# A pitch of 68 KB in place of 64 KB in two DRAM scratch tensors

## The chip, the cores and the metric

The kernel runs on one core of one Trainium2 chip. The metric is the device time of one execution in microseconds, the median of three runs. Lower is better. A profile of one more execution of each kernel gives the spans, the waits and the DMA packets.

## The reference

Each of 8 batches has 3008 rows of 256 numbers. A real Fourier transform runs along the rows, a complex 256 x 256 weight with a bias and a soft threshold is applied to every frequency, and the inverse transform goes back. Then a two-layer network with an ELU follows on all 24064 rows:

```python
X = np.fft.rfft(x, axis=1)
Yr = Xr @ w_r - Xi @ w_i + b_r
Yi = Xr @ w_i + Xi @ w_r + b_i
Yr, Yi = soft(Yr, 0.01), soft(Yi, 0.01)     # sign(v) * max(|v| - 0.01, 0)
y = np.fft.irfft(Yr + 1j * Yi, n=3008, axis=1)
h = y.reshape(24064, 256) @ w_in            # 256 -> 2048
out = elu(h) @ w_out                        # 2048 -> 256
```

## The kernel before

The length 3008 is split as 47 x 64, so each transform is done in two steps of matrix products with a change of layout between them. The layout is changed by way of DRAM: a tile with 128 partitions is stored, and read back with other numbers on the partitions.

For a batch `b` the work is a row of units:

- `unit_A` (6 units of 4 columns j): the first step of the forward transform. `load_x` has brought a third of the batch into `xts[ci]`; two matrix products with `M1` fill PSUM, a copy makes bf16 tile `A`, and a store on the SP queue writes it to the scratch tensor `DA` of shape [24, 128, 256] bf16. One row of 256 is 512 bytes, one j is 64 KB. The stores take 4 j each in batch 0 (line 154) and 8 j later (line 156); every partition writes one 512-byte row for each j.
- `load_Z` reads `DA` back as `Z` with 96 partitions: each j is cut into 4 runs of 32 rows, and every run lands on one partition. The DRAM side folds j and the quarter into one count of 96 with a step of 16 KB. Batch 0 uses four loads of 8 rows per partition (384 KB, pieces of 4096 bytes); the later batches use one of 8 rows and one of 24 rows (1152 KB, pieces of 12288 bytes). Line 163.
- `unit_X` (8 units): the second step, from `Z` and `M2` into `XT`. Units 2g and 2g+1 need rows 8g to 8g+7 of `Z`.
- `unit_M` (12 units) applies the weights, the bias and the threshold; `unit_B` (6 units) is the first step of the inverse transform and stores `Bz` to the scratch tensor `DB`, again [24, 128, 256] (lines 254 and 259).
- `load_Bs` reads `DB` back as four tiles `Bs` of 96 partitions with 8 rows each (384 KB, line 265), and `unit_Y` (8 units, two for each `Bs`) makes the transposed rows `yT` in SBUF.

The network runs over blocks of 512 rows with 8 pairs of 128 hidden columns each, 376 steps in all. A step has `front` (the product with `w_in_s`, line 695, and the exponential), `elu` and `finish_elu` on VectorE, and, two steps later, `back` (the product with `w_out_r`, line 752). After each block the result goes through `osb` to the output (line 770); where the block crosses a quarter of a batch, the store of 16 runs of 8 rows is cut in two, with 14 and 2 runs, 12 and 4, and so on.

The order is written out by hand. Batch 0 goes first, alone, with filler products (`idle_pe`) on TensorE; the A units of batch 1 follow, and its `Z` loads. From then on `plan(b)` gives each step at most one unit of the next batches, behind which the step's own network products stand: the last Y units of batch b, the X, M and B units of batch b+1, the A units of batch b+2, then the loads of `Z` for b+2. Every engine runs its instructions in program order. All scratch stores, scratch loads and output stores are issued on the SP queue in program order too; loads of x and `w_out` go through the GpSimd queue. `gate` holds back the loads of x until a part of `Z` has landed.

The two scratch tensors come from a DRAM pool with two buffers each.

Of the kernel before, what the change touches and what calls it, by code (L numbers as in the profile page):

```python
# [10 lines left out]
BF16 = mybir.dt.bfloat16  # L11
# [10 lines left out]
K1 = 24  # L22
NH = N2 // 2
NJ = 24
# [5 lines left out]
def kernel(  # L30
# [11 lines left out]
    nc = tc.nc  # L42
    P = nc.NUM_PARTITIONS

    B, S, D = x.shape
# [30 lines left out]
    dram = ctx.enter_context(tc.tile_pool(name="dram", bufs=2, space=bass.MemoryType.DRAM))  # L76
# [16 lines left out]
    LAG = 2  # L93
    n = B * PER
    WT = 2 * N1 * 8


    A_of = {}
    DA_of = {}
    Z_of = {}  # L100
# [3 lines left out]
    DB_of = {}  # L104
# [12 lines left out]
    def unit_ps(name, alone):  # L117
        if alone:
            return pre2.tile([P, 2, 512], F32, name=name, tag="pre2")
        return psF.tile([P, 2, 512], F32, name=name, tag="fps")  # L120

    def evac(dst, src, on_dve):
        if on_dve:
            nc.vector.tensor_copy(dst, src)
        else:
            nc.scalar.copy(dst, src)  # L126

    def unit_A(b, u, alone=False, on_dve=False, ahead=False):
        ci, uu = u // 2, u % 2
        if uu == 0:  # L130
            if ahead and ci > 0:
                A_of[b, ci] = late3.tile([P, 8, D], BF16, name="A", tag="gT")
            elif alone:
                A_of[b, ci] = wk4.tile([P, 8, D], BF16, name="A", tag="Bs")
            else:
                A_of[b, ci] = wk2.tile([P, 8, D], BF16, name="A", tag="A")
            if ci == 0:
                DA_of[b] = dram.tile([NJ, P, D], BF16, name="DA", tag="DA")
        xt, A = xts[ci], A_of[b, ci]
        dav = DA_of[b].rearrange("j p d -> p j d")  # L140
        ps = unit_ps("aps", alone or ahead)
        for j in range(2):
            nc.tensor.matmul(  # L143
                ps[:, j, :], lhsT=M1[:],
                rhs=xt[:, 4 * uu + 2 * j : 4 * uu + 2 * j + 2, :], start=True, stop=True,
            )
        evac(
            A[:, 4 * uu : 4 * uu + 4, :].rearrange("p n d -> p (n d)"),
            ps[:].rearrange("p a b -> p (a b)"), on_dve,
        )  # L150
        j0 = 8 * ci
        if alone:
            j0 += 4 * uu
            nc.sync.dma_start(dav[:, j0 : j0 + 4, :], A[:, 4 * uu : 4 * uu + 4, :])
        elif uu == 1:
            nc.sync.dma_start(dav[:, j0 : j0 + 8, :], A[:])

    def load_Z(b, s0, s1):

        if b not in Z_of:  # L160
            Z_of[b] = zp.tile([2 * NR, NS, D], BF16, name="Z", tag="Z")
        dv = DA_of[b].rearrange("j (h c s) d -> (j h c) s d", h=2, c=2)
        nc.sync.dma_start(Z_of[b][:, s0:s1, :], dv[:, s0:s1, :])

    def unit_X(b, u, alone=False, on_dve=False):
        g, dt = u // 2, u % 2
# [60 lines left out]
    def unit_B(b, v, alone=False, on_dve=False):  # L227
        if v % 2 == 0:
            t = "A" if alone and v == 4 else "Bz"
            Bz_of[b, v // 2] = wk2.tile([P, 8, D], BF16, name=t, tag=t)  # L230
            if v == 0:
                DB_of[b] = dram.tile([K1, P, D], BF16, name="DB", tag="DB")
        Bz, Y = Bz_of[b, v // 2], Y_of.pop((b, v))
        ps = unit_ps("bps", alone)
        for pp in range(2):
            for c in range(2):
                for s in range(2):
                    nc.tensor.matmul(  # L238
                        ps[:, s, pp * D : pp * D + D],
                        lhsT=M3[s * N2 : s * N2 + N2, 2 * v + pp, c, :],  # L240
                        rhs=Y[s * N2 : s * N2 + N2, pp, c * D : c * D + D],
                        start=(c == 0), stop=(c == 1),
                    )
        o = 4 * (v % 2)
        Bv = Bz[:, o : o + 4, :].rearrange("p (q s) d -> p s q d", s=2)
        psv = ps[:].rearrange("p s (q d) -> p s q d", d=D)
        if on_dve:
            nc.scalar.copy(Bv[:, :, 0], psv[:, :, 0])
            nc.vector.tensor_copy(Bv[:, :, 1], psv[:, :, 1])
        else:  # L250
            nc.scalar.copy(Bv, psv)  # L251
        if alone:
            k0 = 4 * v
            nc.sync.dma_start(
                DB_of[b][k0 : k0 + 4].rearrange("k p d -> p k d"), Bz[:, o : o + 4, :]
            )
        elif v % 2:
            k0 = 8 * (v // 2)
            nc.sync.dma_start(DB_of[b][k0 : k0 + 8].rearrange("k p d -> p k d"), Bz[:])

    def load_Bs(b, w):

        Bs = wk4.tile([4 * K1, 8, D], BF16, name="Bs", tag="Bs")
        dv = DB_of[b].rearrange("k (c h m) d -> (k c h) m d", c=2, h=2)
        nc.sync.dma_start(Bs[:], dv[:, 8 * w : 8 * w + 8, :])
        Bs_of[b, w] = Bs

    def unit_Y(b, u, alone=False, on_dve=False):
# [6 lines left out]
        for j in range(8):  # L275
# [4 lines left out]
        evac(  # L280
            yT[:, dt, w * WT : w * WT + WT].rearrange("p (r j) -> p r j", j=8),
            psv[:, :, 0 : 2 * N1].rearrange("p j r -> p r j"), on_dve,
# [16 lines left out]
    with tc.tile_pool(name="stagep", bufs=1) as stagep:  # L299
# [186 lines left out]
        def fA(u):  # L486
            unit_A(0, u, alone=True)
            if u < 5:
                idle_pe(3)
# [20 lines left out]
        for g in range(4):  # L510
            load_Z(0, 8 * g, 8 * g + 8)
# [65 lines left out]
    def fB(v, on_dve=False):  # L577
        unit_B(0, v, alone=True, on_dve=on_dve)
# [52 lines left out]
    for h, w in enumerate((w40, w41)):  # L631
        nc.gpsimd.tensor_scalar(
            M4v[:, :, h], r4[0 : 2 * NR], w[0 : 2 * NR], None, ALU.mult
        )
    load_Bs(0, 0)
    load_Bs(0, 1)

    def scale_w_in(q, on_dve):
# [8 lines left out]
    for u in range(6):  # L647
        unit_A(1, u, on_dve=bool(u % 2), ahead=True)
        if u in (1, 3):
            scale_w_in((u + 1) // 2, True)  # L650
            load_Bs(0, 2 + u // 2)
        idle_pe(2)
    scale_w_in(3, False)
    for s0, s1 in ((0, 8), (8, NS)):
        load_Z(1, s0, s1)
# [29 lines left out]
    def front(i, third, on_act):  # L685
        blk, fp = divmod(i, NPAIR)
        if third:
            hps = psF.tile([P, 2, TB], F32, name="hps", tag="fps")
        else:
            hps = psH.tile([P, 2, TB], F32, name="hps", tag="hps")  # L690
        for s in range(2):
            ft = 2 * fp + s
            for b, t0, c0, c1 in pieces(blk * TB, TB):
                for dt in range(2):
                    nc.tensor.matmul(  # L695
                        hps[:, s, c0:c1], lhsT=w_in_s[:, dt, ft * P : ft * P + P],
                        rhs=yT_of[b][:, dt, t0 : t0 + c1 - c0],
                        start=(dt == 0), stop=(dt == 1),
                    )
        Et = late3.tile([P, 2, TB], F32, name="Et", tag="Et")  # L700
        E_ = Et[:]
        if i == n - 1:
            for s in range(2):
                nc.scalar.activation(E_[:, s], hps[:, s], AF.Exp)
        elif on_act:
            nc.scalar.activation(E_, hps[:], AF.Relu, scale=-1.0)  # L706
            nc.scalar.activation(E_, E_, AF.Exp, scale=-1.0)  # L707
        else:
            nc.scalar.activation(E_, hps[:], AF.Exp)  # L709
        return hps, Et  # L710
# [25 lines left out]
    def back(i, split):  # L736
# [24 lines left out]
        for q in range(nq):  # L761
            copy = nc.vector.tensor_copy if (last and q) or (split and q == 0) else nc.scalar.copy
            copy(osb[:, 2 * q : 2 * q + 2, :], po[q][:])
            for i_ in range(2 * q, 2 * q + 2):
                for b, t, c0, c1 in pieces(bs + i_ * P, P):
                    ov = out[b * S : b * S + S, :].rearrange("(r w j) e -> w r j e", w=4, j=8)
                    while c0 < c1:
                        w, r0 = t // WT, t % WT // 8
                        k = min(c1 - c0, (w + 1) * WT - t)
                        (nc.scalar if last and i_ % 2 == 0 else nc.sync).dma_start(  # L770
# [5 lines left out]
    def put(kind, b, *a):  # L776
        return ({"A": unit_A, "X": unit_X, "M": unit_M, "B": unit_B, "Y": unit_Y}[kind], (b, *a))

    def plan(b):
# [18 lines left out]
        for t, u in enumerate(seq, lead):  # L798
            if u[0] == "y":
                f0[t].append(put("Y", b, u[1]))  # L800
            elif u[0] == "n":
                f0[t].append(put("Y", n1, u[1]))
            elif u[0] == "A":
                if n2 < B:
                    f0[t].append(put("A", n2, u[1]))
            else:
                f0[t].append(put(u[0], n1, *u[1:]))
            if u == ("A", 1):
                f1[t] += [(load_Bs, (n1, w)) for w in range(4)]
            if u == ("A", 5) and n2 < B:  # L810
                f1[t] += [(load_Z, (n2, s0, s1)) for s0, s1 in ((0, 8), (8, NS))]
# [9 lines left out]
    for i in range(n + LAG):  # L821
        if i < n:
# [10 lines left out]
            h = front(i, calm and bare % 3 == 2, on_act)  # L833
# [42 lines left out]
```

## Time and profile before

| | |
|---|---|
| median of 3 runs | 923.68 us (922.78 to 924.06) |
| profiled execution | 922.12 us, span 920.3 us |
| granted TensorE clock | 0.997 |
| TensorE busy (matmul) | 897.0 us, 97% of the span |
| VectorE, ScalarE, GpSimd busy | 753.4, 695.0, 263.3 us |
| DMA | 90655 packets, 106.21 MB, mean 115 GB/s |
| loads of `Z` | 7 of 1152 KB, 11 of 384 KB |
| loads of `Bs` | 32 of 384 KB |
| stores to `DA` | 21 of 512 KB, 6 of 256 KB |
| stores to `DB` | 21 of 512 KB, 6 of 256 KB |

The profile is of one execution. Its time is 1.8 us over its span, which goes from the first to the last instruction. Busy shares are averages over the span; a matmul's end is modelled. A DMA share is the mean busy share of the 16 DMA engines of the core. KB are 1024 bytes; GB/s count bytes in powers of ten. A wait is idle time on an engine, named by what ended it.

### The profile page before, as it was taken

Reading aid. Unit: us, or ns where it says so; the run is one execution under the profiler, and the core shown is the slowest. Engines: PE = TensorE matmul, PEld = TensorE weight load, DVE = VectorE, ACT = ScalarE, POOL = GpSimd, SP = SyncE. Lnnn points to the kernel's source line nnn. Section 1 sums busy time; section 2 is a strip of 40 time slices with the busy share of each in tenths; the row PEclk is TensorE's granted clock in tenths of the full one; section 3 lists DMA queues with packets and bytes.
Section 4 is the critical chain, followed back from the end, with each engine's and each line's share of the span. In section 5 each row is a group of like instructions: output and inputs, shape, how many; then the busy total and the mean of one; then the engine's idle time right before and its main releaser. Section 6 shows DMA issues by size and latency. Waiting matters only on the chain.

```text
span 920.3 us, 17019 instructions
## 1 busy us (share of the span) xinstructions
PE 897.0 (97%) x6711; PEld 648.5 (70%) x6711; DVE 753.4 (82%) x880; ACT 695.0 (76%) x767; POOL 263.3 (29%) x344
## 2 busy tenths in 40 slices
PE   8889999999999999999999999999999999999997
PEld 3347667776678676886678766787667867677775
DVE  8778778887788778887788877898778877798997
ACT  6667788777878778788786888778786878666664
POOL 6702430133311441205402153013331044211332
PEclk9999999999999999999999999999999999999999
DMA  8984216621283215723166031842137111421111
GB/s 267 354 255 146 88 47 187 204 69 47 81 229 126 70 47 150 195 92 92 53 200 184 24 107 55 226 142 87 52 96 204 41 30 47 114 57 36 34 37 46
DMA packets 90655, 106.21 MB, mean 115 GB/s; under 512 B 5264, under 2 KB 81296, under 8 KB 87216
## 3 DMA queue, kind: packets, MB, share of 16 engines
q1 hardware_dynamic: 84320, 77.61, 30.1%
q0 software_dynamic: 5968, 27.26, 9.1%
q8 instruction: 52, 0.85, 0.4%
q10 hardware_dynamic: 288, 0.26, 0.1%
q14 instruction: 27, 0.22, 0.1%
HBM read 55.31 MB, written 49.81 MB: 114 GB/s over the span
## 4 chain that ended last, share of the span: by engine, by line
PE 63%; DVE 21%; issue 5%; ACT 5%; DMA 4%; POOL 1%; DVEq 0%; SPq 0%; ACTq 0%; POOLq 0%
PE hps L695 24%; PE ps_o L752 23%; DVE gT L720 11%; PE mps L189 9%; DVE Et L731 4%; ACT Et L709 2%; PE bps L238 2%; DVE gT L722 2%; DVE Et L733 2%; PE xps L174 2%; PE aps L143 2%; PE yps L276 2%; DMA Z<-DA 1%; DMA DA<-A 1%; POOL Et L731 1%
## 5 line engine op out<-in xcount | busy, mean ns | idle before, releaser
L752 PE MATMUL ps_o<-w_out_r,gT 128*128 128x256 f32 x3008 | 473.0, 300 | 0.9 <-DVE gT L720 0.9
L752 PEld LDWEIGHTS ps_o<-w_out_r,gT 128*128 128x128 f32 x3008 | 399.2, 189 | 55.5 <-DVE gT L720 13.2
L695 PE MATMUL hps<-yT,w_in_s 128*128 128x512 bf16 (+7 forms) x1728 | 388.5, 352 | 6.7 <-DVE gT L720 2.5
L709 ACT ACTIVATE Et<-hps 128x1024 f32<-128x1024 f32 x291 | 299.8, 1030 | 84.5 <-PE hps L695 78.0
L720 DVE SCALAR_TENSOR_TENSOR gT<-Et,hps 128x1024 fp32r<-128x1024 f32 (+1 forms) x179 | 216.8, 1212 | 52.8 <-ACT Et L707 36.6
L722 DVE SCALAR_TENSOR_TENSOR gT<-hps,Et 128x1024 fp32r<-128x1024 f32 x198 | 242.0, 1222 | 16.3 <-DVE Et L733 0.5
L695 PEld LDWEIGHTS <-w_in_s 128*128 128x128 bf16 x1728 | 144.2, 98 | 137.3 <-issue 26.9
L733 DVE TENSOR_SCALAR Et<-Et 128x1024 f32<-128x1024 f32 x198 | 136.9, 691 | 45.3 <-ACT Et L709 37.9
L204 POOL TENSOR_SCALAR clip<-yb 128x512 f32<-128x512 f32 x84 | 51.7, 616 | 323.4 <-DVE yb L196 280.0
L706 ACT ACTIVATE Et<-hps 128x1024 f32<-128x1024 f32 x84 | 86.3, 1027 | 72.9 <-PE hps L695 72.4
L731 POOL TENSOR_SCALAR Et<-Et 128x512 f32<-128x512 f32 x94 | 59.8, 637 | 279.3 <-ACT Et L709 278.0
L205 POOL TENSOR_TENSOR Y<-yb,clip 128x512 bf16<-128x512 f32 x84 | 107.2, 1277 | 7.0
L196 DVE TENSOR_TENSOR yb<-mps,bias_bc 128x512 f32<-128x512 f32 x96 | 66.0, 689 | 36.6 <-PE mps L189 30.0
L707 ACT ACTIVATE Et<-Et 128x1024 f32<-128x1024 f32 x84 | 88.8, 1057 | 2.7
L126 ACT CAST XT<-xps 128x768 bf16<-128x768 f32 x61 | 48.7, 800 | 15.6 <-PE xps L174 15.6
L189 PE MATMUL mps<-wcat_r,XT 128*128 128x512 bf16 x192 | 58.8, 388 | 0.9 <-ACT XT L126 0.6
L126 ACT CAST yT<-yps 128x752 bf16<-128x752 f32 x63 | 49.7, 789 | 13.0 <-PE yps L276 12.9
L189 PE MATMUL mps<-wcat_s,XT 128*128 128x512 bf16 x192 | 57.7, 382 | 0.0
L126 ACT CAST A<-aps 128x1024 bf16<-128x1024 f32 x45 | 45.6, 1014 | 16.0 <-PE aps L143 14.4
L731 DVE TENSOR_SCALAR Et<-Et 128x512 f32<-128x512 f32 x94 | 54.1, 576 | 0.9 <-ACT Et L709 0.8
L189 PEld LDWEIGHTS <-XT 128*128 128x128 bf16 x384 | 30.7, 98 | 30.7 <-issue 2.5
L251 ACT CAST Bz<-bps 128x1024 bf16<-128x1024 f32 x46 | 46.0, 1000 | 2.9 <-PE bps L238 2.9
(102 smaller groups left out, 402.4 us busy)
## 6 DMA issues: line engine op xcount, KB each, us to landing
xt<-in_x_dram POOLq DMA_DIRECT2D x21, 1024.0 KB, 5.8
out_dram<-osb SPq DMA_DIRECT2D x158, 128.0 KB
Bs<-DB SPq DMA_DIRECT2D x32, 384.0 KB
DA<-A SPq DMA_DIRECT2D x21, 512.0 KB
DB<-Bz SPq DMA_DIRECT2D x21, 512.0 KB
Z<-DA SPq DMA_DIRECT2D x7, 1152.0 KB
Z<-DA SPq DMA_DIRECT2D x11, 384.0 KB
xt<-in_x_dram POOLq DMA_DIRECT2D x6, 512.0 KB, 6.2
```

What stands on the lines that cost most here:

```text
L126: nc.scalar.copy(dst, src)
L189: nc.tensor.matmul(ps, lhsT=XT[:, dt, c, o : o + P], rhs=wm[:, dt, :], start=(m == 0 and dt == 0), stop=(m == 1 and dt == 1),)
L205: nc.gpsimd.tensor_tensor(Y_of[b, q][:, i, :], yb[:], clip[:], ALU.subtract)
L695: nc.tensor.matmul(hps[:, s, c0:c1], lhsT=w_in_s[:, dt, ft * P : ft * P + P], rhs=yT_of[b][:, dt, t0 : t0 + c1 - c0], start=(dt == 0), sto ...
L706: nc.scalar.activation(E_, hps[:], AF.Relu, scale=-1.0)
L707: nc.scalar.activation(E_, E_, AF.Exp, scale=-1.0)
L709: nc.scalar.activation(E_, hps[:], AF.Exp)
L720: nc.vector.scalar_tensor_tensor(o, e, -1.0, h, ALU.add, ALU.max)
L722: nc.vector.scalar_tensor_tensor(o, h, 0.0, e, ALU.max, ALU.add)
L731: eng.tensor_scalar(E_[:, s], E_[:, s], 1.0, 0.0, ALU.min, ALU.max)
L733: nc.vector.tensor_scalar(E_, E_, 1.0, -1.0, ALU.min, ALU.add)
L752: nc.tensor.matmul(po[q][:, i_ % 2, :], lhsT=gT[:, s, i_ * P : i_ * P + P], rhs=w_out_r[:, ft, :], start=(ft == 0 and i_ % 2 == 0), stop=( ...
```

## The change

Each j of `DA` and each k of `DB` gets 136 rows of 512 bytes in place of 128; the last 8 are never written or read. The views for the stores and loads take rows 0 to 127. For the loads, j and the four quarters can no longer be folded into one count with one step, so the view keeps them apart, as 24 times 4.

```diff
+    PITCH = P + 8
...
-                DA_of[b] = dram.tile([NJ, P, D], BF16, name="DA", tag="DA")
+                DA_of[b] = dram.tile([NJ, PITCH, D], BF16, name="DA", tag="DA")
...
-        dav = DA_of[b].rearrange("j p d -> p j d")
+        dav = DA_of[b][:, 0:P].rearrange("j p d -> p j d")
...
-        dv = DA_of[b].rearrange("j (h c s) d -> (j h c) s d", h=2, c=2)
-        nc.sync.dma_start(Z_of[b][:, s0:s1, :], dv[:, s0:s1, :])
+        dv = DA_of[b][:, 0:P].rearrange("j (q s) d -> j q s d", q=4)
+        nc.sync.dma_start(Z_of[b][:, s0:s1, :], dv[:, :, s0:s1, :])
...
-                DB_of[b] = dram.tile([K1, P, D], BF16, name="DB", tag="DB")
+                DB_of[b] = dram.tile([K1, PITCH, D], BF16, name="DB", tag="DB")
...
-                DB_of[b][k0 : k0 + 4].rearrange("k p d -> p k d"), Bz[:, o : o + 4, :]
+                DB_of[b][k0 : k0 + 4, 0:P].rearrange("k p d -> p k d"), Bz[:, o : o + 4, :]
...
-            nc.sync.dma_start(DB_of[b][k0 : k0 + 8].rearrange("k p d -> p k d"), Bz[:])
+            nc.sync.dma_start(DB_of[b][k0 : k0 + 8, 0:P].rearrange("k p d -> p k d"), Bz[:])
...
-        dv = DB_of[b].rearrange("k (c h m) d -> (k c h) m d", c=2, h=2)
-        nc.sync.dma_start(Bs[:], dv[:, 8 * w : 8 * w + 8, :])
+        dv = DB_of[b][:, 0:P].rearrange("k (q m) d -> k q m d", q=4)
+        nc.sync.dma_start(Bs[:], dv[:, :, 8 * w : 8 * w + 8, :])
```

## The prediction

> **What bounds the kernel now.** I read the page first, then the waits, the chain of waits of the first 80 us, the DMA view, and rates by stretches.
>
> On the page TensorE is busy in 97% of the span. The scratch tensors matter only where TensorE waits for them. The waits, TensorE alone, first for 0 to 80 us, then for 80 to 920 us (who waited, for what: us in total, times, longest):
>
> ```profile
> PE xps L174 <- DMA Z<-DA: 1.8, 4, 1.0
> PE yps L276 <- DMA Bs<-DB: 0.6, 1, 0.6
> ```
> ```profile
> PE yps L276 <- DMA Bs<-DB: 0.9, 1, 0.9
> ```
>
> Six waits, 3.3 us in all: no change of the scratch tensors can gain more through these waits, and the places where a slower load would bite are few. The chain of waits (start us, us, what) shows the loads that lie on the path:
>
> ```profile
> 15.29 3.15 DMA DA<-A
> ...
> 19.39 6.19 DMA Z<-DA
> ...
> 50.06 2.26 DMA DB<-A
> ...
> 52.40 4.14 DMA Bs<-DB
> ...
> 57.78 6.99 DMA DA<-A
> ...
> 64.86 4.38 DMA Z<-DA
> ```
>
> All of them lie before 70 us. Later the loads run ahead: by the DMA packets of the trace the second Z load of batch 2 ends at 168.1 us and its first reader starts at 177.7; the next batches have about 13 us.
>
> The DMA view of the whole run gives counts:
>
> ```profile
> DMA packets 90655, 106.21 MB, mean 115 GB/s; under 512 B 5264, under 2 KB 81296, under 8 KB 87216
> ...
> q1 hardware_dynamic: 84320, 77.61, 30.1%
> ```
>
> How fast the loads run, from stretches (start:end, length, busy time and count of each engine, then clock, DMA share, GB/s). The first two lie in the four Z loads of batch 0, the third in loads of x:
>
> ```profile
> 20.50:22.50 2.00, 1.07 (x5) 0.29 (x3) 1.83 (x5) 0.59 (x2) 2.00 (x2) 1.00 0.99 313
> ...
> 24.50:26.00 1.50, 1.28 (x23) 0.84 (x20) 1.47 (x3) 1.33 (x2) 1.16 (x3) 1.00 1.00 240
> ...
> 30.00:36.00 6.00, 4.27 (x25) 1.83 (x23) 5.67 (x7) 2.89 (x5) 4.80 (x4) 1.00 1.07 427
> ```
>
> The reader should see two things in the last columns. All 16 DMA engines are occupied all the time (share 0.99 to 1.00), so there is no idle engine to take over work; and yet they move only 240 GB/s, where loads of x move 427. The DMA view of 18 to 28 us in 40 slices shows that it comes with the queue:
>
> ```profile
> DMA  9996209567679999998999999999998999999779
> GB/s 352 385 373 230 70 8 197 82 131 147 197 279 393 410 360 311 311 246 246 279 295 262 262 295 246 279 262 246 246 238 189 258 221 287 213 328 274 180 188 180
> ```
>
> The loads begin at 19.5 us and reach 360 to 410 GB/s while the first is moved; from 22 us on the rate is near 250 with the engines as busy. So something slows the chunks of Z. Whether that is the 64 KB pitch, the trace of before can't say.
>
> **The change, part by part.**
>
> *Stores of A and Bz.* Same instructions, same 512-byte pieces, and the outer count is the 128 partitions on both sides. Only the step between a partition's 8 pieces grows from 64 to 68 KB. A lone store moves 275 GB/s at a DMA share of 0.86 (stretch 108.4 to 110.3). I take 0; bounds are 0.3 us either way, a tenth of the 3.15 us store on the chain.
>
> *Space.* 8 rows per 128 that nobody touches: no transfer, no cost.
>
> *Loads of Z and Bs: how the work is dealt out.* Before, j, h and c of the DRAM side fold into one count of 96 with one step of 16 KB, equal to the 96 partitions. After, the step from quarter 3 of a block to quarter 0 of the next differs, so the DRAM side is 24 blocks of 4 quarters. The kernel already has transfers whose DRAM side has an outer count of its own: the shorter stores of osb, 8 each of 112, 96, 80, 64, 48, 32 and 16 KB, with 14, 12, 10, 8, 6, 4 and 2 blocks of 8 rows. The counts show what that does. All data pieces have 512 bytes or more, so the 5264 packets under 512 B are marks at the end of transfers. The DMA issues are 326 on SP, 2 on ACT and 29 on POOL, 357; 16 marks each make 5712. The page has 448 fewer, and that is 8 x (2+4+6+8+10+12+14) exactly. So a transfer leaves one mark on each DMA engine it runs on, the loads of Z and Bs run on 16 now, and a store with r outer blocks in DRAM runs on r engines, although its 112 to 16 SBUF partitions would allow 16. Whole outer blocks are what is dealt out. Of 24 blocks the busiest engine gets two, whether 12 engines have two each or some have one: 8 chunks of the 96, where 6 are the share now. At an unchanged time per chunk a load takes 8/6, a third longer.
>
> [...]
>
> *The price, place by place* (starts from the timeline).
> 1. Z of batch 0: four loads of 384 KB; the X units start at 22.52, 24.11, 25.63 and 27.15 us, one pair per load, each after a wait for Z. A load thus takes 1.52 us. Three of them at a third more: 3 x 0.51 = 1.5. The first runs faster, at about 390 GB/s in the DMA view of 18 to 28 us, so 1.0 us and a third of that, between 0.33 and 0.5: I take 0.4. Sum 1.9 us. The filler matmuls behind each X unit hide nothing, since TensorE waits already.
> 2. Bs of batch 0: TensorE waits 0.6 us for it at 56.59: 0.4.
> 3. Z of batch 1: loads of 384 and 1152 KB, first packet 65.8, last 72.8 us. The first X unit waits at 69.28: 0.4. The third needs the second load; the gate copy shows it landed at 73.29 and the unit starts at 73.57, so 0.28 us is spare. A third of 7.0 us is 2.3, less 0.28: 2.0 at most for both; with the first load's milder price, 1.8.
> 4. Bs of batch 1: TensorE waits 0.9 us at 150.16: 0.4.
> 5. Bs of batch 7: issued at 800.12, first read at 804.62 with no wait. For batch 0 the same way took 52.40 to 56.59, 4.2 us; here there were 4.5. So 0.3 us is spare and 0.1 is left of 0.4.
>
> Issuing costs SP about 0.42 us per load; the stores of osb with an extra count issue every 0.6 to 0.7. The 0.2 us more lie under loads that take 1.5.
>
> Sum: 1.9 + 0.4 + 1.8 + 0.4 + 0.1 = 4.6 us. Nothing gives it back: TensorE runs its program in order and is full to the end. The profiled execution took 922.12 us (span 920.3, 1.8 around it); 4.6 more is 926.7. It lies 1.56 under the median of 923.68, so on the median the forecast is **928.3 us**.
>
> *What the pad may do to the time per chunk.* That is the unknown: from no help (240 GB/s for 16 engines stay 180 for 12) to a rate like x's. The rows set both ends; I take no help, because the first load already starts at 390 GB/s with the same 64 KB pitch and only a longer queue falls to 240. [...]
>
> **The rivals.**
>
> *The limit is shared (925.0).* If 240 GB/s is a ceiling of the whole path and not of each engine, 12 engines move it too, 20 GB/s each; in the loads of x an engine moves 427/16 = 27. Then long queues cost nothing and only the four first loads at fresh speed pay 0.33 each: 1.3 us. For it: all engines slow down together from 390 to 240. Against it: nothing that names the ceiling.
>
> *Not slower: the pitch was the brake.* In step, 16 engines read addresses 16 KB apart; 68 KB breaks that up. At x's 27 GB/s, 12 engines move 320: a Z load takes 1.23 us in place of 1.52. Three loads gain 0.9, the four first loads still lose 1.3, and the second load of batch 1 is hidden: 924.1, no change. It becomes a gain if the blocks are dealt over 16 engines after all: a load then takes 0.92 us, but a pair of X units with its fillers needs about 1.15, so three loads gain 1.1, and with shorter waits of the first loads 1.5 to 2: about 922.0. It decides from a load of under 1.4 us. For it: x at 427 has no such pitch. Against: x also fills 128 partitions, Z 96.
>
> *Twelve engines collide (931).* If what slows the chunks is two engines meeting at one place of SBUF, a new pattern of 12 may meet more often; at half the fastest rate (390/2/16 = 12 GB/s per engine, 146 for 12) a load takes 2.7 us, 1.2 more, and the sum is about 8.
>
> *The change doesn't take effect on the split (923.7).* If single chunks are dealt out, all stays on 16 engines. Against it: the 448 missing marks.
>
> **How the numbers follow.** The forecast has 0.55 (own range 926 to 930), the shared limit 0.17, not slower 0.12, collisions 0.12, no effect 0.04. A measurement can tell about 0.2% from no change, 1.85 us: slower begins at 925.5, faster at 921.8. Slower: 0.55 + 0.12 + a third of the shared limit = 0.73. Faster: the larger part of "not slower", 0.08. The rest, 0.19, is the same. For 8 in 10 the range goes from 923.5 to 931.0; it leaves out most of "not slower" and the upper half of the collisions.
>
> **What would show it.** 50 loads (18 of Z, 32 of Bs) with 12 marks in place of 16: 200 fewer, 5064 packets under 512 B and 84120 on q1. The steps between X pairs of batch 0 go from 1.52 to 2.0 us, the DMA share there to 0.75; the third X unit of batch 1 waits for Z for about 1.4 us. Packets of 4096 bytes that get shorter would mean a shared limit or a pitch that mattered. Counts of 5264 would make the prediction wrong at its root.

## The result, and the profile after

The changed kernel takes 930.4 us (median of 6 runs, 929.3 to 933.78), the kernel before 922.95 us in the same comparison: a ratio of 1.0085 (95% interval 1.0067 to 1.0103), about 7.5 us more. The forecast was 928.3 us, the range 923.5 to 931.0. The profiled execution of the changed kernel took 930.93 us, 8.8 more than the profiled one of before.

Its page, the counts of packets:

```profile
DMA packets 90455, 106.21 MB, mean 114 GB/s; under 512 B 5064, under 2 KB 81096, under 8 KB 87016
...
q1 hardware_dynamic: 84120, 77.61, 29.4%
```

200 packets fewer, with the same bytes: each of the 50 loads of `Z` and `Bs` now leaves 12 marks in place of 16. With one mark for each engine, as the counts of before have it, twelve DMA engines carry them; the DMA share of 0.70 in the changed kernel's stretch of 76 to 80 us, shown further down, fits 12 of 16.

The waits of TensorE for these loads, first 0 to 80 us, then 80 to 920 us (who waited, for what: us in total, times, longest):

```profile
PE xps L175 <- DMA Z<-DA: 5.9, 4, 2.0
...
PE yps L277 <- DMA Bs<-DB: 1.3, 1, 1.3
```
```profile
PE xps L175 <- DMA Z<-DA: 2.3, 1, 2.3
...
PE yps L277 <- DMA Bs<-DB: 1.1, 1, 1.1
```

3.3 us in all became 10.6. The line of 2.3 us after 80 us is the third X unit of batch 1, which waited for nothing before. The chain of waits, the transfers on it:

```profile
15.49 3.22 DMA DA<-A
...
20.63 8.26 DMA Z<-DA
...
54.03 2.27 DMA DB<-A
...
58.57 1.40 SPq L266
...
61.67 2.12 SPq L266
...
63.88 6.72 DMA DA<-A
...
71.50 10.61 DMA Z<-DA
```

The stores take what they took. The loads of `Z` have grown from 6.19 and 4.38 us to 8.26 and 10.61, and the second stretch now reaches to the second load of batch 1. Between the stores to `DB` and `DA` the chain no longer runs through a load of `Bs`, but through the instructions with which SP issues these loads (`SPq L266`).

Where the 8.8 us between the two profiled executions come in, by the starts of units in the two timelines:

| from, to | before | after | more | forecast |
|---|---|---|---|---|
| start to first M unit (`Z` of batch 0) | 29.04 | 33.06 | 4.0 | 1.9 |
| to first Y unit (`Bs` of batch 0) | 27.55 | 28.27 | 0.7 | 0.4 |
| to first X unit of batch 1 | 12.69 | 14.09 | 1.4 | 0.4 |
| to its third X unit | 4.29 | 6.73 | 2.4 | 1.4 |
| to first Y unit of batch 1 | 76.59 | 76.87 | 0.3 | 0.4 |
| to first Y unit of batch 7 | 654.5 | 654.5 | 0.0 | 0.1 |
| to the end | 115.7 | 115.6 | -0.1 | 0 |

The places are the ones named; in this pair of profiles the first and third cost twice and more what was forecast. Theory A says that a chunk (the piece of a load that goes to one partition) costs the same as before and only the share per engine grew. The other theories say that the pitch, the form of the view, a ceiling, or engines that hinder each other change the price of a chunk.

### The profile page after: what moved, and what is told of

The parts are those of the page before. It is cut to its first block, busy times and chain, and to the rows that moved or that the text cites. A ratio compares the mean times of both kernels' runs of the same rounds, so it can differ in the third digit from the quotient of the medians.

```text
span 929.1 us, 16915 instructions
## 1 busy us (share of the span) xinstructions
PE 893.6 (96%) x6607; PEld 649.7 (70%) x6711; DVE 753.3 (81%) x880; ACT 695.1 (75%) x767; POOL 263.0 (28%) x344
## 2 busy tenths in 40 slices
DMA packets 90455, 106.21 MB, mean 114 GB/s; under 512 B 5064, under 2 KB 81096, under 8 KB 87016
## 3 DMA queue, kind: packets, MB, share of 16 engines
q1 hardware_dynamic: 84120, 77.61, 29.4%
## 4 chain that ended last, share of the span: by engine, by line
PE 61%; DVE 20%; issue 6%; ACT 5%; DMA 4%; POOL 1%; SPq 1%; DVEq 0%; ACTq 0%; POOLq 0%
PE hps L696 23%; PE ps_o L753 22%; DVE gT L721 11%; PE mps L190 9%; DVE Et L732 4%; ACT Et L710 2%; PE bps L239 2%; DVE gT L723 2%; DMA Z<-DA 2%; PE xps L175 2%; DVE Et L734 2%; PE aps L144 2%; PE yps L277 1%; DMA DA<-A 1%; POOL Et L732 1%
## 5 line engine op out<-in xcount | busy, mean ns | idle before, releaser
L696 PE MATMUL hps<-yT,w_in_s 128*128 128x512 bf16 (+7 forms) x1653 | 382.3, 351 | 10.7 <-DVE gT L721 2.4
L127 ACT CAST yT<-yps 128x752 bf16<-128x752 f32 x63 | 49.7, 789 | 14.1 <-PE yps L277 13.9
L190 PE MATMUL mps<-wcat_r,XT 128*128 128x512 bf16 x177 | 55.4, 388 | 1.1 <-ACT XT L127 0.7
L190 PE MATMUL mps<-wcat_s,XT 128*128 128x512 bf16 x181 | 55.4, 383 | 0.8
```

The costliest lines, as they stand in the source:

```text
L190: nc.tensor.matmul(ps, lhsT=XT[:, dt, c, o : o + P], rhs=wm[:, dt, :], start=(m == 0 and dt == 0), stop=(m == 1 and dt == 1),)
L696: nc.tensor.matmul(hps[:, s, c0:c1], lhsT=w_in_s[:, dt, ft * P : ft * P + P], rhs=yT_of[b][:, dt, t0 : t0 + c1 - c0], start=(dt == 0), sto ...
```

## The experiments

**Pitch.** `e1_pitch128k` keeps the 24 blocks and takes the 4 KB stagger away:

```diff
-    PITCH = P + 8
+    PITCH = 2 * P
```

> The changed kernel with a pitch of 128 KB per block (128 unused rows) in place of 68 KB: the loads still have 24 outer blocks, the 4 KB stagger is gone. Theory A (the 24 blocks put the loads on 12 DMA engines, the pitch does nothing): about 930.5 us, 5064 packets under 512 B. Theory B (the stagger of 4 KB speeds the chunks and hides part of the cost of 12 engines): 932 to 934 us, packets of 4096 and 12288 bytes longer than in the changed kernel. Theory C (68 KB itself is a bad pitch): 925 us or less.

Measured: 931.4 us, ratio 1.0091 (1.0068 to 1.0114), the same as the changed kernel within the intervals. The packets did get longer, as theory B had it: a median of 914 ns for 12288 bytes, where the four profiled kernels with a 68 KB pitch and uncut 24 x 4 loads of `Z` have 868 to 889. It is too little to tell in the time: 931.4 us lies short of the 932 to 934 of theory B, though the interval reaches into them. `e2_fold96_15k` is the other half: 16 engines, but a step that is no power of two.

```diff
-        dv = DA_of[b].rearrange("j (h c s) d -> (j h c) s d", h=2, c=2)
-        nc.sync.dma_start(Z_of[b][:, s0:s1, :], dv[:, s0:s1, :])
+        v = DA_of[b].rearrange("j p d -> (j p) d")
+        dv = bass.AP(tensor=v.tensor, offset=v.offset + s0 * D,
+                     ap=[[30 * D, 96], [D, s1 - s0], [1, D]])     # the same for Bs
+        nc.sync.dma_start(Z_of[b][:, s0:s1, :], dv)
```

> The kernel before, with the loads of Z and Bs taking 96 chunks at a step of 15 KB in place of 16 KB: same bytes and one outer count of 96, but rows that overlap, so Z and Bs hold other data. Theory A: 16 engines, 5264 packets under 512 B, and 923 us as before. Theory B (power-of-two steps slow the chunks): the packets of 12288 bytes fall from about 795 ns towards 480 ns and the time to 921 to 922 us.

Measured: 922.17 us, ratio 0.9999 (0.9989 to 1.0008), and the median packet of 12288 bytes took 798 ns, as before. So another step does not help a load here, and the stagger is worth at most the few per cent of a packet just named: the pitch was not the brake.

**Form of the view.** `e3_48blocks` has a view that can't be folded, but with 48 blocks in place of 24, three for each of 16 engines: `ap=[[62 * D, 48], [32 * D, 2], [D, s1 - s0], [1, D]]`.

> The kernel before, with loads that view DRAM as 48 blocks (62 rows apart) of 2 chunks: it can't be folded, like the changed kernel's 24 x 4, but 48 and 96 allow 16 engines. The data differ. Theory A in its pure form (only the number of engines costs): 5264 packets under 512 B and 923 us. Rival D (the unfolded view itself costs: SP issues a load in 0.78 us in place of 0.42, and the first packet comes later): issue 0.78 us, and 3 to 4 of the 7.5 us, 926 to 927 us.

Measured: 922.73 us, ratio 1.0004 (0.9995 to 1.0014). SP needs 0.59 us per load (median), between 0.42 (loads of `Z` before) and the 0.78 of the changed kernel, and the end does not move. Up to that price, the form alone costs less than the comparison can tell. Rival D at its full 0.78 us was not reached by this run; what SP's time costs comes up again below, with `e10` and `e12`.

**Number of engines.** `e4_8blocks` and, later, `e8_6blocks` use the same form with 8 blocks of 12 chunks (`[380 * D, 8], [32 * D, 12]`) and 6 blocks of 16 (`[508 * D, 6], [32 * D, 16]`).

> The kernel before, with loads that view DRAM as 8 blocks (380 rows apart) of 12 chunks. The data differ. Theory A: 8 engines with 12 chunks each, 400 marks fewer than before (4864 packets under 512 B); at an unchanged time per chunk a load takes twice as long as before, three times the added part of 12 engines, so 937 to 945 us. Rival E (a shared ceiling near 240 GB/s sets the rate of long queues): 8 engines at 25 GB/s still reach 200, and the time is 931 to 934 us.

Measured: 933.61 us, ratio 1.012 (1.0105 to 1.0135), 4864 packets under 512 B. The time is at rival E's, under theory A's, but a ceiling does not explain the packets. Stretches in the `Z` loads of batch 1 of four kernels, where nothing else is moved (length, busy times, clock, DMA share, GB/s): before, changed, 8 blocks and 6 blocks. The stretch of 8 blocks still holds the last packets of the first load; the row under it, from the second load alone, gives the same picture:

```profile
68.50:71.00 2.50, 2.16 (x21) 1.58 (x21) 2.25 (x3) 1.68 (x3) 0.00 (x0) 1.00 0.98 236
```
```profile
76.00:80.00 4.00, 3.82 (x31) 2.99 (x30) 1.92 (x2) 3.61 (x4) 0.00 (x0) 1.00 0.70 169
```
```profile
77.00:81.00 4.00, 2.39 (x15) 1.64 (x16) 0.47 (x1) 1.13 (x2) 0.00 (x0) 0.77 0.53 218
...
79.00:82.00 3.00, 3.00 (x15) 2.24 (x12) 0.27 (x1) 1.83 (x2) 0.00 (x0) 0.53 0.49 205
```
```profile
94.00:100.00 6.00, 2.14 (x17) 1.56 (x14) 3.00 (x3) 1.83 (x2) 0.00 (x0) 0.98 0.27 82
```

Divide GB/s by 16 times the DMA share, and the rate of a busy engine comes out: 15.1 before, 15.1 in the changed kernel, 25.7 and 26.1 with 8 blocks, 19.0 with 6. Eight engines move more in all (205 to 218 GB/s) than twelve (169). A ceiling on the whole can't do that. A price per chunk that is fixed whatever the number of engines can't either: by the packet records 12288 bytes took, as a median over all seven such loads, 798 ns with 16 engines, 868 with 12 and 462 with 8. Rival E falls, and theory A falls as a general rule; for the step from 16 to 12 engines its price is nearly right.

What is left to try is which partitions are written at the same time. A packet record names neither its engine nor its partition, so no trace shows that directly. The shares of slow packets show that it is not a few engines alone: of the packets of 12288 bytes only 6% took under 600 ns in the changed kernel and 10% in the kernel before, against 80% with 8 engines. The next runs change the number of engines, or the partitions that one load covers.

`e8_6blocks` has fewer engines than 8. (From here on the expectations call the ceiling S; E is a fixed price per chunk.)

> The kernel before, with loads that view DRAM as 6 blocks (508 rows apart) of 16 chunks; the data differ. 6 engines. [...] Theories E with a ceiling and S: fewer engines than 8 can't be slower per chunk, so 460 ns throughout and 7.7 us.

Measured in one execution, the profiled one, of 962.73 us: 4764 packets under 512 B, 500 fewer than before, so 6 engines; per busy engine 19.0 GB/s (the row above) in place of 25.7; of the packets of 12288 bytes 36% took under 600 ns and 44% took 800 or more, where with 8 engines 80% were under 600. The loads took 12 to 17.5 us. The five longest ran beside loads of x; the `Z` load of batch 1, with nothing beside it, took 12.2 us, more than the 7.7 of theories E and S, and its packets have a median of 597 ns. Fewer engines, and each is slower (19.0 against 25.7 GB/s): neither a ceiling nor a fixed price says that, and this run does not show what does.

**Each load cut in two.** `e5_12eng_halves` cuts each load of the changed kernel at block 12:

```diff
-        nc.sync.dma_start(Z_of[b][:, s0:s1, :], dv[:, :, s0:s1, :])
+        for j0, j1 in ((0, 12), (12, 24)):     # the same for Bs
+            nc.sync.dma_start(Z_of[b][4 * j0 : 4 * j1, s0:s1, :], dv[j0:j1, :, s0:s1, :])
```

> The changed kernel with each load of Z and Bs cut in two at block 12: partitions 0 to 47, then 48 to 95, both on 12 engines with 4 chunks each. [...] Theory E (a chunk costs the same whatever is beside it, only the share per engine counts): packets stay near 870 ns in both halves, loads at 7.5 us or more, and the kernel at 930 to 932 us. Theory S (a shared ceiling): as E.

Measured: 927.52 us, ratio 1.005 (1.0035 to 1.0066), clear of the 930 to 932 of E and S. The loads of 1152 KB took 6.0 to 7.3 us, less than the 7.5 of E. Their packets, in four quarters by time, have medians of 774, 953, 575 and 462 ns in batch 1, where nothing else was moved (825, 933, 517 and 462 in batch 3): slow in the first half, fast at the end, with the same pitch and 12 blocks in each half (a store of `osb` with 12 blocks left 12 marks). A price per chunk that is the same whatever is beside it does not fit these medians.

`e6_pad_cut32` is the same with `((0, 8), (8, 24))`: 8 blocks, then 16, where the load of 8 blocks (e4) and the stores of `osb` with 16 left 8 and 16 marks.

> The changed kernel with each load cut at block 8: partitions 0 to 31 on 8 engines (4 chunks each), then 32 to 95 on 16 engines (4 chunks each). [...] Theory E: busiest engine has 8 chunks as in the changed kernel, so nothing is won and the kernel stays at 929 to 932 us.

Measured: 923.57 us, ratio 1.0014 (1.0006 to 1.0023). All but 1.1 us of the loss is gone, with the pad in place. A stretch in the `Z` loads of batch 1, with the end of the first:

```profile
70.00:73.00 3.00, 2.94 (x28) 2.04 (x25) 2.67 (x4) 2.31 (x3) 0.00 (x0) 1.00 0.88 302
```

302 GB/s where the kernel before has 236; the median packet took 461 ns. The loads of 1152 KB took 4.45 to 6.5 us, where the changed kernel needs 7.6 on average. From the first Y unit to the first X unit of batch 1 this kernel needs 14.3 us, as the changed kernel does (14.1): the cut does not win back that row of the table.

**Can the cut beat the kernel before?** `e7_nopad_cut32` cuts the unpadded loads at partition 32, `e11_cut_Z0_later` only the second to fourth `Z` load of batch 0:

```diff
-        nc.sync.dma_start(Z_of[b][:, s0:s1, :], dv[:, s0:s1, :])
+        for q0, q1 in ((0, 32), (32, 96)) if b == 0 and s0 else ((0, 96),):   # e7: always, and Bs too
+            nc.sync.dma_start(Z_of[b][q0:q1, s0:s1, :], dv[q0:q1, s0:s1, :])
```

> The kernel before, without a pad, with each load cut at partition 32: 32 partitions on 16 engines (2 chunks each), then 64 on 16 (4 chunks each). [...] Theory E or S: same packets of about 790 ns, and 922.4 to 924 us.

Measured: 923.31 us, ratio 1.0011 (1.0003 to 1.002). The median packet fell to 561 ns. In the 1152 KB load of batch 1 the quarters by time have medians of 612, 858, 468 and 460 ns, with the 16 KB step of the kernel before throughout: the step stays, and the partitions of a load change. (That the parts of 32 and 64 chunks have 16 engines each, as the 96 had, is the author's estimate.) Still the kernel is not faster: with two issues of 0.53 us per load the first X unit starts at 23.17 in place of 22.53, and the pairs are 1.5 to 1.8 us apart.

> The kernel before, with only the second, third and fourth load of Z of batch 0 cut at partition 32 (32 partitions, then 64); the first load, all of Bs and the later batches are uncut. [...] Rival (SP's two issues per load, 1.06 us, and the fillers set the pace): steps of 1.5 us and 922.5 or more.

Measured: 923.66 us, ratio 1.0017 (1.0008 to 1.0026); pairs 1.76, 1.60 and 1.54 us apart. The steps and the time are the rival's, but its cause is not shown by this run: here the packets of the cut loads did not get faster. Those of 4096 bytes, taken 96 at a time in order of start, have medians of 302, 294 and 283 ns for the second to fourth load, where the kernel before has 220, 228 and 257. Why stays open. No version tried beats the kernel before.

**Which tensor.** `e10_pad_DA_only` leaves `DB` and the loads of `Bs` as before.

> Only DA gets the pad and the 24 x 4 view; DB and the loads of Bs are as before. 72 marks fewer than before (5192 packets under 512 B). By the traces of before and after, 4.0 us come in up to the first M unit and 3.8 with Z of batch 1, 0.7 with Bs of batch 0 and 0.2 with Bs of batch 1: so 929 to 930 us. Rival (the loads of Bs hold up the stores behind them on SP's queue and cost more than their own waits): 927 to 928 us.

Measured: 927.01 us, ratio 1.0052 (1.0038 to 1.0066). `DB` thus has 0.33% of the 0.85%, about 3 us, although the waits for `Bs` grew only from 1.5 to 2.4 us. SP's issues in the changed kernel (start us, us, what) show where it goes:

```profile
58.06 0.46 SPq L157 DMA_DIRECT2D DA<-A  x1
58.57 1.40 SPq L266 DMA_DIRECT2D Bs<-DB  x1
60.07 1.55 SPq L157 DMA_DIRECT2D DA<-A  x1
61.67 2.12 SPq L266 DMA_DIRECT2D Bs<-DB  x1
63.88 0.49 SPq L157 DMA_DIRECT2D DA<-A  x1
```

And in the kernel before:

```profile
53.73 0.57 SPq L265 DMA_DIRECT2D Bs<-DB  x1
54.40 0.91 SPq L156 DMA_DIRECT2D DA<-A  x1
55.36 2.33 SPq L265 DMA_DIRECT2D Bs<-DB  x1
57.78 0.93 SPq L156 DMA_DIRECT2D DA<-A  x1
```

The last tile `A` of batch 1 is ready at 60.15 us and its store goes out 3.7 us later; in the kernel before 1.6 us later (56.19 and 57.78). `Z` of batch 1 waits for that store. The other profiles agree: from the first Y unit to the first X unit of batch 1 the changed kernel, `e1` and `e9` need 14.1 to 14.4 us, and `e10`, with the old loads of `Bs`, needs 12.9; before it was 12.7. `e12_Bs_behind_A` moves the third and fourth `Bs` load behind the stores:

```diff
         if u in (1, 3):
             scale_w_in((u + 1) // 2, True)
-            load_Bs(0, 2 + u // 2)
         idle_pe(2)
     scale_w_in(3, False)
+    for w in (2, 3):
+        load_Bs(0, w)
```

> The changed kernel with one thing moved: the third and fourth load of Bs of batch 0 are issued behind the three stores of A of batch 1 instead of between them (and ahead of the Z loads, which wait for the last store anyway). In the changed kernel SP is busy with these loads for 1.40 and 2.12 us, and the last store of A goes out at 63.88 us, 2.55 us after the first Y unit starts, where before it was 1.19. Theory Q (the store waits in SP's program order behind the dearer loads, and that is the 1.4 us by which Z of batch 1 comes later than its own loads explain): the last store goes out about 1.2 to 2 us earlier against the first Y unit, the step from the first Y unit to the first X unit of batch 1 falls from 14.1 us to 12.3 to 12.9, kernel 928.6 to 929.3. Rival (the DMA queue and not SP's order sets when the store is done): no change, 930.4.

```profile
55.34 1.57 SPq L266 DMA_DIRECT2D Bs<-DB  x2
57.02 5.14 SPq L157 DMA_DIRECT2D DA<-A  x3
62.21 2.24 SPq L266 DMA_DIRECT2D Bs<-DB  x2
66.46 1.55 SPq L164 DMA_DIRECT2D Z<-DA  x2
```

The last store on its chain of waits:

```profile
59.19 7.20 DMA DA<-A
```

Measured: 927.15 us, ratio 1.0048 (1.0035 to 1.0061): 3 us won back, twice what theory Q said. The last store starts to be issued at 59.19 us, 0.07 us after its tile, and first Y to first X of batch 1 is 12.35 us. The store itself takes no less than before (7.20 us against 6.72), so it is its earlier start that gains. The further gain lies in the next row of the table: the third X unit comes 5.8 us after the first, not 6.7. Whether the kernel before would gain by the same move was not tried.

**Clock.** In the profiled execution of the changed kernel the granted clock of TensorE (third column from the end) was at half for 3.4 us from 27.1 us on, while X units ran:

```profile
28.00:29.50 1.50, 1.16 (x16) 1.03 (x15) 0.00 (x0) 1.17 (x2) 1.50 (x4) 0.50 1.06 231
```

`e9_more_filler` fills the waits with products:

```diff
-    idle_pe(34)
+    idle_pe(42)
...
-        idle_pe(1)
+        idle_pe(6 if u in (1, 3) else 1)
```

> The changed kernel with more filler products on TensorE where it waits for Z of batch 0: 42 in place of 34 before the first X unit, 6 in place of 1 behind the X units 1 and 3. They lie in waits of 2.0, 1.8 and 0.3 us. Theory G (the longer waits let the granted TensorE clock fall to half for 3.4 us from 27.1 us on, while X and M units run, and that is about 1 us of the added 7.5): no half-clock stretch before 36 us, last X unit to first M unit back from 2.25 to 1.85 us, kernel 929.0 to 929.8 us. Rival (the clock stretch lies beside waits for Z anyway): 930.4 us or more.

Measured: 930.33 us, ratio 1.0087 (1.0074 to 1.01): no gain. Its profiled execution had no half-clock stretch before 925 us, its first M unit at 31.01 us and 928.9 us in all, but the median stands where it stood. Theory G is not borne out in the time. The profiles do differ with the clock: `e1` and `e12`, with a half-clock stretch among the X units like the changed kernel (33.06 us), have their first M unit at 32.28 and 32.02 us, while `e10`, whose loads up to there are the changed kernel's, had none and has it at 30.55, 1.5 us later than before and not 4.0. So a good part of the first row of the table belongs to that one execution; what such stretches do to the median stays open.

## Why the prediction was right or wrong

- *Twelve engines*: right, to the packet (5064 and 84120). That 24 blocks would take exactly twelve was the author's estimate: no run of before shows a count of 24. The runs showed 12 engines for 24 blocks (200 marks fewer than before), 8 for 8 (400 fewer, e4) and 6 for 6 (500 fewer, e8); with 48 blocks the time was that of 16 engines (922.73 us, e3).
- *The places, and that nothing gives it back*: right. From the first Y unit of batch 1 on, the two traces run in parallel.
- *Pad, stores and pitch at nothing*: right in the time (e1, e2; 3.22 against 3.15 us for the store on the chain). That a 64 KB pitch has nothing to restore was the author's estimate, from a first load that starts at 390 GB/s with that pitch; e2 agrees (798 ns for 12288 bytes at a step of 15 KB, as at 16).
- *A load takes 8/6*: right in size, by luck in its reason. The seven loads of 1152 KB took 7.6 us on average in place of 5.9, a ratio of 1.30, and a busy engine moved 15.1 GB/s in both kernels (stretches above). The steps between X pairs of batch 0, forecast at 2.0 us, were 3.1, 2.1 and 1.9 in the changed kernel's profile. But the "unchanged time per chunk" is no constant: with 8 engines it was 462 ns in place of 798. It came out alike for 16 and 12 (means of 775 and 828 ns for 12288 bytes, 249 and 229 for 4096) because both splits happen to be slowed alike. The shorter packets of 4096 bytes were the prediction's own sign for a shared limit or a pitch that mattered; e4 speaks against the limit, e1 and e2 against a pitch that shows in the time.
- *The 240 against 427 GB/s*: the gap was seen and its cause was left open between the pitch and the 96 partitions. e2 speaks against the pitch and e7 for the partitions, in the kernel before too: cut at partition 32, the same loads fell to 460 ns in their second part (612 and 858 in the first). How the partitions do this no run shows.
- *Issuing lies under the loads*: wrong, and by e12 the largest miss. An issue was forecast at 0.6 to 0.7 us and was 0.78 (median; up to 2.1), and its price is not under the load it issues but on the store behind it in SP's order: 1.4 us in the third row, where 0.4 was forecast, and about 3 us with what follows (e10, e12). With the order changed, 4.4 us of loss are left (e12), close to the 4.6 of the sum.
- *First load 0.4*: at the low end. The first X unit came 1.3 us later in the changed kernel's profile, with the first packet 1.7 us after SP began the issue in place of 1.0; the four other profiles with these loads have 0.4 to 1.1.

The range held the result by 0.6 us. The median moved by 7.5 us where 4.6 were forecast, and the case held to be likeliest had its own range of 926 to 930, missed by 0.4 us. The rival "twelve engines collide" was priced at 931, next to the 930.4 measured, but that is luck: it wanted a busy engine to fall to 12 GB/s, where 15.1 were measured, and its sum had nothing for SP's order.

## What to carry to other kernels

When a view of DRAM stops folding into the partition count, look up its outer count before anything else: here it set how many DMA engines carried the load (16 with 96 chunks, 12 with 24 blocks, 8 with 8, 6 with 6), and a pad that was to cost nothing but space cost a quarter of them and 7.5 us. Fewer engines were not slower in proportion (8 moved 205 to 218 GB/s, 12 moved 169): which partitions a load covers changed as much here (953 ns for 12288 bytes in one half of e5's load, 462 at the end of the other), and one cut at partition 32 won back all but 1.1 us of the loss. And a dearer issue on SP's queue was paid by the store behind it (about 3 us, e12), so ask who waits for that.

## What the runs showed that was not expected

In the stretches shown, eight DMA engines moved 205 to 218 GB/s into 96 partitions where twelve moved 169 and sixteen 236. Cut at partition 32, with 8 engines and then 16, the load ran at 302. SP's issue of a `Z` load cost 0.42 us with a folded view, 0.59 with 48 blocks, 0.78 with 24 blocks on 12 engines (medians); with several loads on the way single issues took up to 2.3 us in the kernel before as well, and what holds SP there was not tried.
